# Channel attention with a routed expert layer on one core: squares of the next batch's first products behind the third routing step's row numbers, and its bias table one routing step earlier

## The chip, the cores and the metric

The kernel runs on one core of a Trainium2 chip. The metric is the device time of one execution in microseconds (us), from launch to end. The kernel before has three timed runs: 1178.34, 1178.45 and 1178.51 us, a median of 1178.45 us. A further execution was recorded by the hardware profiler; all rows of the trace below come from it.

The engines of the core are named as the profile names them: PE multiplies matrices (PEld is its loading of weights), DVE and ACT work element by element, POOL starts the indirect DMAs, and SP starts all other DMAs. Each engine has a queue of its own instructions, and engines wait for each other through semaphores.

## What is computed

The reference is a channel attention over four batches, followed by a mixture of eight experts with one expert for each token. Cut to what matters:

```python
# q, k, v: (4, 5056, 256)
qn = q / (norm(q, axis=1) + 1e-6);  kn = k / (norm(k, axis=1) + 1e-6)
a = softmax(kn.transpose(0, 2, 1) @ qn / tau)      # (4, 256, 256)
x = (v @ a).reshape(20224, 256)
logits = x @ w_gate + modality_bias[modality_id]   # 8 experts
e_idx = argmax(logits); gate = softmax(logits)[e_idx]
out[t] = gate[t] * (relu(x[t] @ w1[e]) @ w2[e])    # e = e_idx[t], hidden size 1024
```

## The kernel before

A batch's 5056 tokens are cut into ten steps of 512 tokens (the last is shorter). Three kinds of work run over these steps.

**Products.** For each batch the 256x256 product k'q is summed in one PSUM tile (`g`, L368) over the ten steps, from loads of q and k. Beside it the squares of q and k are summed for the norms: ACT squares a half step into `sq` (L347), DVE adds it to `acc` (L349). In a step there are four such pairs, q and k of two halves. A function `kq_pieces(b, s, behind, later)` hands out one step. With a list given as `later`, the squares aren't put out there and then but collected in that list, and are put out when the main loop runs the list; and with `behind`, each of them is ordered on its engine behind the instructions that `behind` names. Batch 0's product fills the first 45 us; batch 1's steps are spread over batch 0's routing steps, and so on.

**Routing steps.** There are 40, numbered g = 0 to 39, ten in a batch. A step turns v (L570 on PE for the first six steps; a DMA that transposes, L537 into `T`, then four DMAs into planes `pl`, L514, and joining copies into `vt`, L521 and L522, for the later ones), splits it into a high and a low part (`vh` on ACT, L574; `vl` on DVE, L575), multiplies it by the attention in four tiles of 128 tokens (`xp`, L588), copies the result into rows `x` (L595, L599, L600) and adds the bias table `bsel` to the logits (L601). Then DVE finds each token's expert, PE makes prefix sums over the tokens (`rp`, L646 and L647), and DVE works out each token's row number (`pi`, L660). POOL scatters the rows into a DRAM buffer `xs` that is sorted by expert, four indirect DMAs a step (L477). The scatters of steps 3 and 4 are held until the fourth tile of the next step has been copied (`HELD`).

**Blocks.** A block is 512 rows of one expert, and there are 40 here. After each routing step from g = 2 on (except one) DVE picks a block from the counts (`pick`, L700 to L730). Its weights are loaded on SP (`w1r`, `w2r`, two halves each), its rows are read back from `xs` by a transposing DMA (`Tx`, L769), joined into `xt` (L521, L522) and split into `xh` (ACT, L833) and `xl` (DVE, L834). PE multiplies by w1 (`hp`, L848) and w2 (`y`, L869), each as three products of high and low parts. Block 0 (called slot 0) needs the rows of steps 0, 1 and 2; `START = 2` is the index of the last of these.

What sets the order: the Python loops hand out pieces, a helper deals the pieces of several streams out in proportion, and when the program is built a scheduler lays each engine's instructions out in one fixed order, by when it reckons each to be ready. `order(ins, others)` adds that one instruction stands behind others on its queue. On the chip, each queue keeps that order.

Around the change: batch 1's product steps 0 and 1 are put out before routing step 0, step 2 beside routing step 1. Their squares in the kernel before: step 0's at once; step 1's after routing step 0, behind its row numbers (`routed[0]`: on DVE the numbers at L660 and the gate at L666, on ACT the copy of the token numbers at L662); step 2's after routing step 1, behind `routed[1]`. `setup_bias` makes a batch's bias table from the modality of each token in three operations on DVE (L262 twice, L267); for batch 1 it is put out after routing step 7 (`NS // 2 + 2` with NS = 10), behind that step's numbers.

Of the kernel before, what the change touches and what calls it, by code (L numbers as in the profile page):

```python
# [20 lines left out]
def _interleave(*streams):  # L21

    lists = [list(s) for s in streams if len(s) > 0]
    total = [len(x) for x in lists]
    at = [0] * len(lists)
    while any(a < n for a, n in zip(at, total)):
        i = min(
            (i for i in range(len(lists)) if at[i] < total[i]),
            key=lambda i: ((at[i] + 0.5) / total[i], i),
        )  # L30
        lists[i][at[i]]()
        at[i] += 1
# [3 lines left out]
def kernel(  # L36
# [15 lines left out]
    B, N, C = q.shape  # L52
# [4 lines left out]
    NS = -(-N // STEP)  # L57
# [19 lines left out]
    START = 2  # L77
# [103 lines left out]
    def pad_rows():  # L181

        ins = nc.sync.dma_start(
            xs[E * CAP : E * CAP + BLK, :].rearrange("(p t) c -> p t c", t=BLK // P),
            pad[0].bitcast(I32).unsqueeze(1).to_broadcast([P, BLK // P, XW]),
        )
        pads.append(ins.ins)
        tc.declare_no_dep(
            ins.ins, group="xr", reason="no expert has rows there"
        )  # L190
# [283 lines left out]
    routed = {}  # L474
# [20 lines left out]
    def slots_by(g):  # L495

        return max(0, g + 1 - START - sum(x <= g for x in SKIP))

    def lag(g):

        n = LAG
        for x in SKIP:
            n -= g >= x + n
        return n
# [424 lines left out]
    def run(pieces):  # L929
        for f in pieces:  # L930
            f()
# [19 lines left out]
    def once(blk, what):  # L951
        key = (blk["slot"], what)
        if key not in done:
            done.add(key)
            run(blk[what])

    def block_stream(blk, nxt):

        once(blk, "load")
        once(blk, "prep")  # L960
        body = list(blk["body"])
        if nxt is not None:
            once(nxt, "load")
            done.add((nxt["slot"], "prep"))
            split0, turn, split1 = nxt["prep"]
            for o, f in reversed(list(zip((7, 10, 13), (split0, lambda: turn(blk["evicted"][NJ - 3]), split1)))):
                body.insert(o, f)
        before = open_blk[0]["last"] if open_blk[0] is not None else []
        for i, f in enumerate(open_blk[0]["stores"] if before else []):
            blk["beside"].setdefault(2 + i, []).append(f)  # L970
        open_blk[0] = blk
        if not before:
            return [blk["first"]] + body
        return [blk["first"], before[0], body[0]] + before[1:] + body[1:]
# [17 lines left out]
    def ask(n):  # L992
        if n < len(tasks) and n not in loaded:
            loaded.add(n)
            product(n)[0]()

    def products_of(g):

        out = []
        for n, (at, b, i) in enumerate(tasks):  # L1000
            if at == g:
                out += [lambda n=n: ask(n)] if g <= first_block else []
                out += product(n)[1:]
                if g >= first_block and (b, i) != (1, NS - 1):
                    out.append(lambda n=n: ask(n + (1 if g == first_block else 2)))
        if g == first_block + 1:
            out.append(lambda: ask(min(n for n in range(len(tasks)) if tasks[n][0] > g) + 1))
        return out
# [1 line left out]
    va = [va_pieces(*divmod(g, NS)) for g in range(G)]  # L1010
    va[0][2]()
    run(va[0][0])
    squares = {1: [], 2: []}
    for s in BEFORE:
        if s == 0:
            run(kq_pieces(1, s))
        else:
            run(kq_pieces(1, s, lambda: routed[0], squares[s]))
    pad_rows()
    for g in range(G):  # L1020
        b, s = divmod(g, NS)
        streams = []
        for gg, blk in waiting:
            if gg <= g + 1 - lag(g + 1):
                once(blk, "load")
        if len(waiting) > 0 and waiting[0][0] <= g - lag(g):
            _, blk = waiting.pop(0)
            streams.append(block_stream(blk, waiting[0][1] if waiting and waiting[0][0] <= g + 1 - lag(g + 1) else None))
        soft = list(softmax_pieces(b)) if s == 0 and b > 0 else []
        begun = []  # L1030
        if g + 1 == first_block:
            split0, turned, split1 = waiting[0][1]["prep"]
            done.add((0, "prep"))
            begun = [split0, split1]
        own = list(va[g][1])
        if g - 1 in HELD:
            t = HELD[g - 1]
            own.insert(t + 1, lambda: va[g - 1][4]([copied[g, t]]))
        turn = []
        if g + 1 < first_block:  # L1040
            turn.append(va[g + 1][2])
        turn += va[g + 1][0] if g + 1 < G else []
        if g + 1 == first_block:
            turn.append(va[g + 2][2])
        if g == first_block:
            turn.append(va[g + 2][2])
        if first_block <= g + 2 < G:
            turn.append(va[g + 2][3])
        if g + 3 == first_block or first_block + 2 < g + 3 < G:
            turn.append(va[g + 3][2])  # L1050
        if g < first_block:
            streams.append(soft + turn + begun + own)
        else:
            streams.append(soft + own[:2] + turn[:1] + own[2:5] + turn[1:] + own[5:])
        if b + 1 < B:
            if b == 0 and s == 1:
                streams.append(list(kq_pieces(1, 2, lambda: routed[1], squares[2])))
            else:
                streams.append(products_of(g))
        _interleave(*streams)  # L1060
        if waiting and waiting[0][0] <= g + 1 - lag(g + 1):
            blk = waiting[0][1]
            once(blk, "load")
            if blk["slot"] == 0:
                turned(blk["evicted"][-1])
            once(blk, "prep")
        if s == NS // 2 + 2 and b < B - 1:
            setup_bias(b + 1, routed[g])
        n = slots_by(g)
        while chosen < n:  # L1070
            waiting.append((g, block_pieces(g, chosen, pick(g, chosen, False), False)))
            chosen += 1
        run(squares.get(g + 1, []))
        if g == NS - 1:
            ask(min(n for n in range(len(tasks)) if tasks[n][0] > g) + 1)
# [84 lines left out]
```

## Time and profile before

| what | value |
|---|---|
| time, median of 3 runs | 1178.45 us |
| time of the profiled execution | 1175.55 us |
| span of the profiled execution, first to last instruction | 1173.7 us |
| PE busy | 1153.6 us (98%) |
| DVE busy | 920.8 us (78%) |
| ACT busy | 806.1 us (69%) |
| POOL busy | 384.7 us (33%) |
| granted TensorE clock, mean | 0.995 |

The span leaves out 1.85 us of the profiled execution's time (1175.55 less 1173.7), and that execution took 2.9 us less than the median run. A difference in the span is carried over to the median as it is. In the rows, "start" and lengths are in us, counted from the first instruction; brackets give how long the engine was idle before the row and what ended that. A busy PE isn't a PE at full speed, since a matmul's time includes waiting in the pipeline; how many matmuls start in a stretch tells more. The clock that PE was granted is in a row of its own, in tenths.

### The profile page before, as it was taken

The numbers are of one execution on the slowest core, as the hardware profiler recorded it, in microseconds if no ns is written. First come the engines' busy times: TensorE is split into PE (matmuls) and PEld (weight loads), VectorE is DVE, ScalarE is ACT, GpSimd is POOL, SyncE is SP. The second block draws the span as 40 slices with busy tenths as digits, with TensorE's granted clock in tenths as the row PEclk, the third lists the DMA queues.
The fourth block names the chain that finished last, engine by engine and source line by source line (L and its number), as shares of the span: only waits on it lengthen the run. The fifth ranks groups of instructions, "written<-read, shape, count | busy, mean of one in ns | idle before, by whom it ended". The sixth has DMA issues, their size and how long they took to land.

```text
span 1173.7 us, 23358 instructions
## 1 busy us (share of the span) xinstructions
PE 1153.6 (98%) x7708; PEld 1054.6 (90%) x7708; DVE 920.8 (78%) x2591; ACT 806.1 (69%) x1655; POOL 384.7 (33%) x345
## 2 busy tenths in 40 slices
PE   8998999999999999999999999999999999999997
PEld 7896989999999999999999999999999999999997
DVE  6787989898888888888888888878777776686552
ACT  6676867877777777687777677767656666556553
POOL 0053333323333332333333333333333333344122
PEclk9998999999999999999999999999999999999999
DMA  8979999688777677759777776765876665464421
GB/s 293 307 236 230 269 239 255 173 248 217 199 200 201 196 192 206 208 159 234 204 209 203 210 202 162 167 182 158 207 218 172 187 176 158 134 178 136 136 86 35
DMA packets 285843, 228.38 MB, mean 195 GB/s; under 512 B 185064, under 2 KB 243944, under 8 KB 285712
## 3 DMA queue, kind: packets, MB, share of 16 engines
q1 hardware_dynamic: 270032, 185.19, 60.3%
q0 software_dynamic: 15680, 41.61, 10.4%
q8 instruction: 62, 1.02, 0.4%
q14 instruction: 69, 0.57, 0.2%
HBM read 128.79 MB, written 43.43 MB: 147 GB/s over the span
## 4 chain that ended last, share of the span: by engine, by line
PE 84%; issue 6%; DMA 5%; POOL 2%; DVE 2%; ACT 1%; SPq 0%; POOLq 0%; DVEq 0%; ACTq 0%
PE y L869 34%; PE hp L848 33%; PE xp L588 9%; PE g L368 6%; DMA k<-in_k_dram 2%; POOL out_dram L477 2%; DMA q<-in_q_dram 1%; DMA Tx<-xs 1%; DMA xs<-x,pi 0%; DMA pl<-T 0%; PE vtp L570 0%; PE gw L437 0%; ACT xt L521 0%; SPq L305 0%; PE atp L431 0%
## 5 line engine op out<-in xcount | busy, mean ns | idle before, releaser
L869 PE MATMUL y<-w2h,hh 128*128 128x256 f32 x1256 | 354.5, 282 | 0.0
L869 PE MATMUL y<-w2l,hh 128*128 128x256 f32 x1256 | 351.2, 280 | 0.0
L869 PE MATMUL y<-w2h,hl 128*128 128x256 f32 x1256 | 349.4, 278 | 0.1
L477 POOL DMA_INDIRECT xs<-x,pi x160 | 196.7, 1229 | 364.0 <-DVE pr L711 183.4
L477 POOL DMA_INDIRECT out_dram<-yo,gt x158 | 174.2, 1103 | 392.1 <-ACT hh L851 297.6
L848 PE MATMUL hp<-xh,w1h 128*128 128x512 f32 (+1 forms) x640 | 250.7, 392 | 5.6 <-ACT xh L833 5.6
L848 PE MATMUL hp<-xl,w1h 128*128 128x512 f32 (+1 forms) x640 | 250.7, 392 | 0.0
L848 PE MATMUL hp<-xh,w1l 128*128 128x512 f32 (+1 forms) x640 | 249.5, 390 | 0.0
L852 DVE SCALAR_TENSOR_TENSOR hl<-hp,hh 128x512 fp32r<-128x512 f32 (+1 forms) x320 | 216.7, 677 | 36.3 <-ACT hh L851 34.6
L869 PEld LDWEIGHTS y<-w2h,hh 128*128 128x128 f32 x1256 | 236.4, 188 | 9.3
L869 PEld LDWEIGHTS y<-w2l,hh 128*128 128x128 f32 x1256 | 236.4, 188 | 8.5
L851 ACT ACTIVATE hh<-hp 128x512 fp32r<-128x512 f32 (+1 forms) x320 | 188.7, 590 | 69.2 <-PE hp L848 69.0
L869 PEld LDWEIGHTS y<-w2h,hl 128*128 128x128 f32 x1256 | 235.3, 187 | 0.4 <-DVE hl L852 0.3
L814 ACT CAST w1h<-w1r 128x512 fp32r<-128x512 f32 x160 | 99.4, 621 | 166.4 <-PE hp L848 165.6
L821 DVE TENSOR_TENSOR w1l<-w1r,w1h 128x512 fp32r<-128x512 f32 x160 | 109.8, 686 | 91.1 <-ACT w1h L814 90.4
L848 PEld LDWEIGHTS hp<-xh,w1l 128*128 128x128 f32 x640 | 120.6, 188 | 26.0
L848 PEld LDWEIGHTS hp<-xh,w1h 128*128 128x128 f32 x640 | 120.4, 188 | 19.5 <-ACT xh L833 5.8
L848 PEld LDWEIGHTS hp<-xl,w1h 128*128 128x128 f32 x640 | 120.8, 189 | 13.4
L821 DVE TENSOR_TENSOR w2l<-w2r,w2h 128x512 fp32r<-128x512 f32 x160 | 109.8, 686 | 12.6 <-ACT w2h L814 11.3
L814 ACT CAST w2h<-w2r 128x512 fp32r<-128x512 f32 x160 | 100.8, 630 | 21.7 <-PE y L869 20.1
L588 PE MATMUL xp<-ah,vh 128*128 128x264 f32 x320 | 92.7, 291 | 0.1
L600 DVE COPY x<-xp 128x256 uint16<-128x256 uint16 x136 | 56.9, 419 | 45.5 <-ACT x L599 45.1
(161 smaller groups left out, 1817.1 us busy)
## 6 DMA issues: line engine op xcount, KB each, us to landing
w1r<-in_moe_w_dram SPq DMA_DIRECT2D x80, 512.0 KB, 4.7
w2r<-in_moe_w_dram SPq DMA_DIRECT2D x80, 512.0 KB, 4.6
q<-in_q_dram SPq DMA_DIRECT2D x35, 512.0 KB, 9.4
k<-in_k_dram SPq DMA_DIRECT2D x35, 512.0 KB, 5.5
pl<-T SPq DMA_DIRECT2D x120, 128.0 KB, 4.6
v<-in_v_dram SPq DMA_DIRECT2D x6, 512.0 KB
xs<-x,pi POOLq DMA_INDIRECT x160, 4.8
out_dram<-yo,gt POOLq DMA_INDIRECT x158, 3.2
```

Of the source, the lines that this page charges most:

```text
L368: nc.tensor.matmul(gram[b][:, m, :], x, y, start=first and m == 0 and i == 0, stop=last and i == len(seq) - 1, skip_group_check=True,)
L477: ins = nc.gpsimd.indirect_dma_start(out=dst, out_offset=bass.IndirectOffsetOnAxis(ap=idx, axis=0), in_=rows, in_offset=None, bounds_check ...
L588: nc.tensor.matmul(xp[:, 0:DE], a[:, h, t * P : (t + 1) * P], w[:, h, :], start=i == 0, stop=i == len(seq) - 1,)
L600: copied[g, t] = nc.vector.tensor_copy(planes[:, 0, :], halfwords[:, 0, :]).ins
L814: ins = nc.scalar.copy(hi, src).ins
L821: evicted[-1] = [ins, nc.vector.tensor_tensor(lo, src, hi.bitcast(F32), ALU.subtract).ins]
L848: nc.tensor.matmul(hp[:, 0:rows], w[:, h, fs], x[:, h, 0:rows], start=i == 0, stop=i == len(seq) - 1)
L851: relu = nc.scalar.activation(hh[:, 0:rows], hp[:, 0:rows], AF.Relu).ins
L852: low = nc.vector.scalar_tensor_tensor(hl[:, 0:rows], hp[:, 0:rows], 0.0, hh[:, 0:rows].bitcast(F32), ALU.max, ALU.subtract).ins
L869: ins = nc.tensor.matmul(y, a[:, tsl], w[:, j % 2, :], start=(j == 0 and i == 0 and t % per == 0), stop=(j == NJ - 1 and i == 2), skip_gro ...
```

## The change

Three places of the main program are edited. The squares of batch 1's product steps 1 and 2 go into one list that is run after routing step 2 (`START`), and all eight pairs are ordered behind step 2's numbers in place of step 0's and step 1's. Batch 1's bias table is put out after routing step 6 in place of step 7; the other batches' stay.

```diff
-    squares = {1: [], 2: []}
+    squares = {START + 1: []}
     for s in BEFORE:
         if s == 0:
             run(kq_pieces(1, s))
         else:
-            run(kq_pieces(1, s, lambda: routed[0], squares[s]))
+            run(kq_pieces(1, s, lambda: routed[START], squares[START + 1]))
...
             if b == 0 and s == 1:
-                streams.append(list(kq_pieces(1, 2, lambda: routed[1], squares[2])))
+                streams.append(list(kq_pieces(1, 2, lambda: routed[START], squares[START + 1])))
...
-        if s == NS // 2 + 2 and b < B - 1:
+        if s == (NS // 2 + 1 if b == 0 else NS // 2 + 2) and b < B - 1:
             setup_bias(b + 1, routed[g])
```

No instruction is added or taken away on any engine. But the scheduler lays out the stretch from routing step 0 to the fourth block anew, so more moves than the diff names. Three places matter below. In the names, the numbers behind a tile are first what it belongs to and last a running number of the build (`rp_2` is routing step 2's, `xp_3_0` is tile 0 of step 3, `pl_7` and `vt_7` are step 7's planes and their joined copy, `Tx_0`, `xt_0` and `xh_0` belong to slot 0, `hl_1_0` to slot 1, `bsel_1` and `btmp_1` to batch 1).

On PE, step 2's prefix sums stood in this place, within the fourth tile of step 3:

```order
L588 MATMUL xp_3_3_915<-ah_0_440,vh_3_749 128x264
L588 MATMUL xp_3_3_915<-al_0_441,vh_3_749 128x264
L646 LDWEIGHTS trim_93
L646 MATMUL rp_2_819<-chosen_of_98,trim_93 128x40
L588 MATMUL xp_3_3_915<-ah_0_440,vl_3_750 128x264
L647 LDWEIGHTS onesb_86
L647 MATMUL rp_2_819<-run_2_814,onesb_86 128x40
```

and now they stand behind the first tile of step 3:

```order
L588 MATMUL xp_3_0_884<-ah_0_440,vl_3_726 128x264
L368 MATMUL g_1_487<-q_1_3_860,k_1_3_862 128x256 x2
L646 LDWEIGHTS trim_93
L646 MATMUL rp_2_795<-chosen_of_98,trim_93 128x40
L368 MATMUL g_1_487<-q_1_3_860,k_1_3_862 128x256
L647 LDWEIGHTS onesb_86
L647 MATMUL rp_2_795<-run_2_790,onesb_86 128x40
```

Seventeen matmuls of step 3 and most of the product matmuls of batch 1's step 3 have moved behind the prefix sums.

On ACT, where slot 0's rows are joined and split, the order was

```order
L521 COPY xt_0_0_1270<-Tx_0_1133 128x512
L521 COPY xt_0_1_1275<-Tx_0_1133 128x512
L595 COPY x_5_991<-xp_5_3_1206 128x512
L833 CAST xh_0_1268<-xt_0_0_1270 128x512
L662 COPY x_5_991<-tokid_100 128x4
L833 CAST xh_0_1268<-xt_0_1_1275 128x512
```

and is now

```order
L521 COPY xt_0_0_1270<-Tx_0_1133 128x512
L521 COPY xt_0_1_1275<-Tx_0_1133 128x512
L521 COPY vt_7_0_1394<-pl_7_1157 128x512
L595 COPY x_5_991<-xp_5_3_1206 128x512
L662 COPY x_5_991<-tokid_100 128x4
L833 CAST xh_0_1268<-xt_0_0_1270 128x512
L833 CAST xh_0_1268<-xt_0_1_1275 128x512
```

A copy of routing step 7's planes has come in ahead of slot 0's split. Before, it stood 13 instructions behind the second `xh`. On SP the DMAs from slot 0's `Tx` to these planes stand in the same order in both kernels.

On DVE, the bias table stood behind step 7's numbers, seventeen instructions ahead of the low halves (`qs`, L324) of batch 1's product step 6:

```order
L660 TENSOR_REDUCE pi_7_2044<-pos_7_2041 128x4
L262 SCALAR_TENSOR_TENSOR bsel_1_2072<-m1_131,mb_sb_263 128x320
L262 SCALAR_TENSOR_TENSOR btmp_1_2073<-m1_131,mb_sb_263 128x320
L711 SCALAR_TENSOR_TENSOR pr_5_2078<-pr_5_2078,prio9_115 128x9
L575 TENSOR_TENSOR vl_9_2216<-vt_9_0_2219,vh_9_2215 128x512
L267 TENSOR_TENSOR bsel_1_2072<-bsel_1_2072,btmp_1_2073 128x320
```

and now stands behind step 6's, among the sums of squares of product step 4:

```order
L660 TENSOR_REDUCE pi_6_1634<-pos_6_1631 128x4
L262 SCALAR_TENSOR_TENSOR bsel_1_1662<-m1_131,mb_sb_263 128x320
L262 SCALAR_TENSOR_TENSOR btmp_1_1663<-m1_131,mb_sb_263 128x320
L705 TENSOR_TENSOR pr_4_1668<-end9_124,nxt9_121 128x9
L349 TENSOR_TENSOR acc_1_488<-acc_1_488,sq_1_4_0_k_1685 128x2x256
L267 TENSOR_TENSOR bsel_1_1662<-bsel_1_1662,btmp_1_1663 128x320
```

The three operations have moved 64 instructions forward on DVE.

## The prediction

> **What bounds the kernel now.** I read the page's slices first, which show PE full nearly everywhere, then busy times by stretch around the slices that fall short, then PE's waits, then the chain of waits around the one place where PE stops. The busy times (start and end, length, then busy us and count for PE, PEld, DVE, ACT, POOL, then granted clock, DMA share, GB/s):
>
> ```profile
> 54.00:92.90 38.90, 38.73 (x263) 35.10 (x261) 31.21 (x142) 28.41 (x63) 16.46 (x16) 1.00 0.73 213
> 92.90:105.00 12.10, 6.52 (x23) 4.88 (x22) 5.27 (x31) 5.10 (x12) 4.36 (x4) 0.72 1.05 250
> 105.00:200.00 95.00, 93.17 (x631) 84.80 (x630) 86.17 (x239) 75.78 (x156) 34.26 (x26) 1.00 1.03 257
> 200.00:1085.00 885.00, 884.92 (x6019) 811.40 (x6018) 717.92 (x2019) 620.53 (x1278) 308.06 (x267) 1.00 0.70 190
> ```
>
> From 200 to 1085 us PE is never idle, so what happens earlier shifts the end one to one: a microsecond at the first block is a microsecond of the time. PE's own waits between 40 and 200 us (total, times, longest) name the two that count:
>
> ```profile
> PE hp L848 <- ACT xh L833: 5.6, 1, 5.6
> PE g L368 <- DVE qs L324: 1.6, 2, 1.1
> ```
>
> The first is slot 0's start, the second comes at 155 to 160 us. The chain of waits leads to the first:
>
> ```profile
> 57.21 0.87 PE vtp L570 x8
> 58.08 1.45 PE xp L588 x12
> 59.53 0.43 PE g L368 x2
> ...
> 68.39 0.44 PE vtp L570 x4
> 68.82 3.46 PE g L368 x16
> ...
> 72.52 0.72 PE xp L588 x6
> ...
> 82.39 5.62 DMA xs<-x,pi
> ...
> 98.62 1.22 PE hp L848 x2
> ...
> 100.50 3.41 PE hp L848 x8
> ```
>
> PE's matmuls pace routing step 2 (the six at 72.52 are its fourth tile), its scatters follow, slot 0's rows come back through `Tx`, and `hp` starts at 98.62.
>
> **Step 2's numbers come earlier.** The sums stood in DVE's queue right behind step 0's and step 1's numbers:
>
> ```profile
> 57.86 0.17 DVE L601 TENSOR_TENSOR L<-xp,bsel 128x8 f32<-128x8 f32 x1 [0.75 <-ACT x L595]
> ...
> 60.85 0.21 DVE L660 TENSOR_REDUCE pi<-pos 128x4 int32<-128x32 f32 x1
> 60.98 0.68 DVE L349 TENSOR_TENSOR acc<-acc,sq_q 128x512 f32<-128x512 f32 x1
> ...
> 77.56 0.20 DVE L660 TENSOR_REDUCE pi<-pos 128x4 int32<-128x32 f32 x1
> ```
>
> Eight sums at 0.60 from start to start are 4.8 us of DVE, and they go behind the last of these rows. But PE set the pace, so I count PE. From 59.53 to the end of step 2's fourth tile (72.52 + 0.72 = 73.24) it took 13.7 us. In the new order 16 product matmuls (3.46 by the row at 68.82), 36 of `xp` (1.45 / 12 = 0.121 each, 4.36), 8 transposes (0.88) and two prefix pairs (0.23 each, an estimate from the chain's 0.43 for two product matmuls) stand in between: 9.15, so the tile ends at 68.7. From there to the numbers step 0 took 61.06 - 57.21 = 3.85 (its fourth tile ended where the chain goes on with the transposes; a copy and the L row follow), with one low half in between as here. So step 2's numbers are done at 72.55 instead of 77.76, 5.2 us earlier. If DVE still lags by a low half or two, it is 4.0; if the prefix sums wait for nothing, 5.6.
>
> The scatters follow on POOL, 0.78 behind the numbers' end:
>
> ```profile
> 78.54 0.98 POOL L477 DMA_INDIRECT xs<-x,pi  x1 [3.58 <-ACT x L662]
> ```
>
> They start 1.28 apart (the chain's 82.39 is the fourth), and by the same count step 1's have left POOL by 72.7, so nothing stands in front. The load of q and k for product step 5 reuses the buffer of step 1, now waits for step 1's squares (some 72 us by this count), and holds its place on SP ahead of slot 0's weights; it needs 1 MB of the DMA engines in a stretch that has room (0.73 above). I cost it at nothing, and at 1 us if that room is gone. `Tx` is then issued at 83.5 instead of 88.72.
>
> **But ACT has a new wait ahead of `xh`.** ACT's queue now holds the copy of step 7's planes between `xt_0` and `xh_0`. What that copy waits for stands on SP behind `Tx`, in the same order as before:
>
> ```profile
> 88.72 2.43 SPq L769 DMA_TRANSPOSE Tx<-xs  x1
> ...
> 93.08 5.84 SPq L537 DMA_TRANSPOSE T<-in_v_dram  x1
> ...
> 101.05 2.65 SPq L514 DMA_DIRECT2D pl<-T  x4
> ```
>
> ```profile
> 97.48 0.57 ACT L595 COPY x<-xp 128x512 uint16<-128x512 uint16 x1
> 97.94 0.62 ACT L833 CAST xh<-xt 128x512 fp32r<-128x512 f32 x1
> 98.46 0.20 ACT L662 COPY x<-tokid 128x4 int32<-128x4 int32 x1
> 98.56 0.62 ACT L833 CAST xh<-xt 128x512 fp32r<-128x512 f32 x1
> ...
> 108.07 0.76 ACT L521 COPY vt<-pl 128x512 uint16<-128x512 uint16 x1
> 108.70 0.62 ACT L347 ACTIVATE sq_q<-q 128x512 f32<-128x512 f32 x1
> ```
>
> The copy needs the third and fourth of the plane DMAs, which started at 102.4 and 103.0; the trace has their landing at
>
> ```profile
> DMA to landing us min/median/max: 4.5/5.1/5.8
> ```
>
> so not ahead of 107.5, and at 108.07 ACT read them without a wait. I take 107.8: 19.1 us behind `Tx`'s issue. In the new order that is 83.5 + 19.1 = 102.6. Then come the copy (0.63 to the next row), `x` (0.46), the token numbers (0.10) and `xh` to `hp` (98.62 - 97.94 = 0.68): `hp` starts at **104.5 instead of 98.62, 5.9 us later**. Behind the waiting copy on ACT stand also `x_5` (on which the held scatters of step 4 wait) and all of slot 0's relu; on DVE the logits of step 5. What is late next after the gain of 5.2 is thus the planes, by far: `Tx` itself would allow 93.4. ACT does stand still for planes already, in the waits from 105 to 200:
>
> ```profile
> ACT vt L521 <- DMA pl<-T: 4.9, 2, 2.8
> ```
>
> The unknown is how long `T` takes to land with its surroundings changed. From its issue to the first plane DMA it was 5.6 (55.12 to 60.73), 8.0 (93.08 to 101.05) and 10.5 (111.00 to 121.46):
>
> ```profile
> 55.12 3.18 SPq L537 DMA_TRANSPOSE T<-in_v_dram  x1
> ...
> 60.73 0.65 SPq L514 DMA_DIRECT2D pl<-T  x1
> ```
>
> ```profile
> 111.00 5.99 SPq L537 DMA_TRANSPOSE T<-in_v_dram  x1
> ...
> 121.46 2.58 SPq L514 DMA_DIRECT2D pl<-T  x4
> ```
>
> I take 8.0, the row in the same place, and keep -2.4 and +2.5 for the range. `T` is half a megabyte. The Trainium skill ("DMA: Bandwidth & Descriptors", Latency and other measured facts) gives transposing DMAs 261 GB/s. By that the half megabyte would need an estimated 2 us, `hp` would start some 6 us sooner than in my sum, and the change would come out near no change. The rows, at three to five times that, don't bear it out; it is weighed with the second rival.
>
> **The slow start after the gap.** The eight `hp` matmuls at 100.50 take 3.41 us, 0.43 each. At full clock it is 0.23:
>
> ```profile
> 108.48 1.38 PE hp L848 x6
> ```
>
> Twelve or so go at the slow rate after the gap, which costs 2.4 us. The gap grows here, but the ramp is paid once either way, so I put it at nothing. The Trainium skill ("TensorE: Matmul & The Clock Gate", Part 1) has the clock halve after an idle window of about 3.4 us and come back after as much sustained work, whatever the idle time. By that rule the ramp would go only where the gap falls under that window, which is the first rival's case; the granted 0.72 in the second row of the busy times agrees with it.
>
> **The bias table.** Its three operations stood just where PE waits for `qs`:
>
> ```profile
> 151.79 0.48 DVE L262 SCALAR_TENSOR_TENSOR bsel<-m,mb_sb 128x320 f32<-128x320 f32 x1
> 152.19 0.48 DVE L262 SCALAR_TENSOR_TENSOR btmp<-m,mb_sb 128x320 f32<-128x320 f32 x1
> ...
> 153.28 0.48 DVE L267 TENSOR_TENSOR bsel<-bsel,btmp 128x320 f32<-128x320 f32 x1
> 156.06 0.67 DVE L324 TENSOR_TENSOR qs<-q,qs 128x512 fp32r<-128x512 f32 x1
> ```
>
> Without them `qs` comes 1.2 us sooner (3 x 0.40 from start to start), off a wait of 1.6 us. I take -1.2. At most the 1.6 go; at worst the three delay a low half of slot 1 by 1.2 where DVE is nearly full (86.17 of 95), which would give +1.2.
>
> **The sum.** +5.9 - 1.2 = +4.7 on a span of 1173.7. Carried to the median of the runs, 1178.45 (the profiled execution itself has 1175.55), that is 1183.1. Ends: 5.9 - 0.4 - 2.4 - 1.6 = +1.5, and 5.9 + 1.2 + 1.0 + 2.5 + 1.2 = +11.8, if all ends meet.
>
> **Rivals.**
> - *The planes aren't late, and the gain of step 2 goes through.* It decides at 96.7: planes that land by then leave `hp` no later than before. Then `hp` starts between 93.4, where `Tx` allows it and PE's earlier work just ends, and about 96, since the eight sums now delay steps 3 and 4; the ramp of 2.4 may go too. With the bias that is -3.8 to -8.8; I take -6, 1172.4. For it speaks that the scheduler put the copy there as ready; against it, that `T` is issued behind `Tx` and no row has planes landing sooner than 10.1 after `T`'s issue (5.6 + 4.5), which from `T` at 87.9 gives 98. Chance 0.08.
> - *The wait is there but short.* `T` lands in 5.6 as in its first row, the planes in 4.5: `hp` 2.9 later, less 1.2 for the bias, +1.7, 1180.2: within 0.2%. 0.14, the skill's rate included.
> - *It goes on.* The held scatters of step 4 start behind `x_5` at about 104, the last of them 3.9 later, and with 5.6 to land like the chain's they are there at 113; `Tx` of slot 2, which needs them, now stands on SP ahead of q and k for product step 6, so SP stands still until then. If that and a slow `T` (+2.5) add up, +9, 1187.5. 0.06.
>
> **How the numbers follow.** The forecast has 0.72; the likeliest time is its 1183.1. About 0.2%, or 2.4 us, is what a measurement of this kernel tells from no change. Slower by more than that: 0.72 + 0.06 = 0.78; within it 0.14; faster 0.08. The range of 8 in 10 leaves out the first rival and the very ends: 1179.5 (the short wait) to 1187.5.
>
> **What would show it.** In the new profile: step 2's `pi` at 72.5, `Tx` issued at 83.5, ACT idle for some 10 us with `vt <- pl` behind it, PE waiting for `xh` until 104.5 with a clock of 0.7 or less, and the `qs` wait under 0.6. Wrong would be: `Tx` not earlier (then the sums were never in the way, and the loss nears 10), planes landed ahead of `xt`, or a new PE wait after 105.

## The result, and the profile after

The changed kernel takes 1185.63 us, the median of six runs (1184.35 to 1187.87); the kernel before, timed beside it, takes 1178.48 us (six runs, 1174.66 to 1178.67). The ratio is 1.0068, with a 95% interval of 1.0053 to 1.0083: slower, by 7.15 us from median to median. The profiled execution of the changed kernel took 1185.73 us with a span of 1183.9, which is 10.2 us more than the span before.

First PE's waits between 40 and 400 us in the changed kernel (total, times, longest):

```profile
PE hp L848 <- ACT x L662: 7.1, 1, 7.1
PE rp L646 <- DVE chosen_of L622: 3.6, 2, 2.6
PE xp L588 <- issue: 2.5, 2, 2.2
PE rp L647 <- DVE run L632: 0.5, 1, 0.5
```

The wait for `qs` is gone, as foretold. The wait ahead of `hp` is there and larger. Two new ones stand before it in time: `rp`, for 1.0 us in routing step 2 and 2.6 in step 4, and `xp` in step 2 (`issue` means that the profile shows nothing the engine waited for; `remote`, further down, that it doesn't know who ended the wait). The chain from `Tx` to `hp` on SP, ACT and PE (start, length, engine, line; in brackets the idle time before the row and what ended it):

```profile
89.92 2.29 SPq L769 DMA_TRANSPOSE Tx<-xs  x1
...
95.11 4.59 SPq L537 DMA_TRANSPOSE T<-in_v_dram  x1
...
103.90 2.60 SPq L514 DMA_DIRECT2D pl<-T  x4
...
108.95 0.76 ACT L521 COPY vt<-pl 128x512 uint16<-128x512 uint16 x1 [9.56 <-DMA pl<-T]
109.58 0.57 ACT L595 COPY x<-xp 128x512 uint16<-128x512 uint16 x1
...
110.28 1.13 ACT L833 CAST xh<-xt 128x512 fp32r<-128x512 f32 x2
...
110.95 1.22 PE L848 MATMUL hp<-xh,w1h 128*128 128x512 f32 x2 [7.05 <-ACT x L662]
```

ACT stands still for 9.56 us with step 7's planes copy at the head of its queue and slot 0's `xh` behind it. `hp` starts at 110.95 instead of 98.62, 12.3 us later. But `Tx` was to be issued earlier than before, at 83.5, and is issued 1.2 us later, at 89.92. Step 2's numbers are the reason:

```profile
78.27 0.21 DVE L660 TENSOR_REDUCE pi<-pos 128x4 int32<-128x32 f32 x1
```

They end at 78.48, where 72.55 was forecast and the kernel before had 77.76. PE lost the time on the way. Busy times by stretch, in the columns of the prediction, of the changed kernel:

```profile
66.00:78.00 12.00, 8.49 (x51) 7.35 (x49) 5.07 (x22) 6.02 (x14) 4.94 (x6) 0.86 0.44 137
...
100.00:112.00 12.00, 4.95 (x21) 4.44 (x21) 3.28 (x21) 3.02 (x8) 2.37 (x4) 0.50 0.90 221
```

and of the kernel before in the first of these stretches:

```profile
66.00:78.00 12.00, 11.97 (x86) 11.05 (x86) 10.08 (x49) 8.90 (x23) 5.18 (x5) 1.00 0.69 227
```

In the 12 us from 66 on, PE started 51 matmuls instead of 86, DVE was busy for half as long and ACT for two thirds. No engine was full there. PE, ACT and POOL of the changed kernel around that gap:

```profile
66.62 0.28 PE L588 MATMUL xp<-ah,vl 128*128 128x264 f32 x1
...
68.08 0.28 PE L588 MATMUL xp<-ah,vl 128*128 128x264 f32 x1
70.52 0.39 PE L588 MATMUL xp<-ah,vh 128*128 128x264 f32 x1 [2.16 <-issue]
```

```profile
69.68 0.58 ACT L595 COPY x<-xp 128x512 uint16<-128x512 uint16 x1 [2.83 <-PE xp L588]
72.53 0.58 ACT L595 COPY x<-xp 128x512 uint16<-128x512 uint16 x1 [2.27 <-PE vtp L570]
74.00 1.07 ACT L595 COPY x<-xp 128x512 uint16<-128x512 uint16 x2 [0.88 <-PE vtp L570]
```

```profile
62.33 1.15 POOL L477 DMA_INDIRECT xs<-x,pi  x1 [51.02 <-DVE pi L660]
...
71.48 0.98 POOL L477 DMA_INDIRECT xs<-x,pi  x1 [0.30 <-issue]
```

and POOL of the kernel before, where step 1's scatters begin:

```profile
69.85 1.27 POOL L477 DMA_INDIRECT xs<-x,pi  x1 [2.71 <-DVE acc L349]
```

The matmul at 66.62 is the last of step 2's first tile, and it ends at 66.90. ACT had been idle for 2.83 us when it began to copy that tile at 69.68. The next two tiles ended at 67.64 and 68.36 and were copied at 72.53 and 74.00, with ACT idle before each. In steps 0 and 1 such a copy starts 0.04 us behind its last matmul. Here three copies in a row are 2.8, 2.3 and 0.9 us late, counted from the tile's end or, where ACT was still busy, from when it came free (the expectations below count from when ACT could have started its next copy, and have 2.4 and 1.0). PE can't go on until the tiles are free, and so lies idle too. The trace's semaphore events say the same of the signals themselves: PE's signals for the three tiles reached the counter at 69.66, 72.51 and 73.97, and three more, of matmuls that ended at 71.52, 72.19 and 73.05, followed from 74.05 to 74.17. The ends of matmuls are modelled in the profile, so it can't be told whether the results were late or only the signals; "late signals" below stands for both. Beside it, POOL issues eight scatters without a pause, those of steps 0 and 1, from 62.33 to 72.46. In the kernel before there were four, a pause of 2.7 us, and four more.

The table sets the places that count side by side for all kernels of this study (end of step 2's numbers, `Tx` of slot 0 issued, first `hp`, span, all in us of one profiled execution; the ratio is that of the timed runs to the kernel before on the same chip). Its median there was 1177.27 us beside the runs from bias_alone to step2_alone, 1177.52 beside those down to before_step0_held and 1175.26 beside the last four, each group on another chip, so kernels of different groups are compared by their ratios and not by their times. One of the twelve runs of bias_planes9 took 1975.24 us at a granted clock of 0.655, and the ratio leaves it out.

| kernel | numbers | `Tx` | `hp` | span | ratio (95%) |
|---|---|---|---|---|---|
| before | 77.76 | 88.72 | 98.62 | 1173.7 | 1 |
| after | 78.48 | 89.92 | 110.95 | 1183.9 | 1.0068 (1.0053 to 1.0083) |
| bias_alone | 77.63 | 88.46 | 96.56 | 1176.5 | 1.0014 (1.0003 to 1.0025) |
| squares_alone | 78.39 | 89.92 | 110.00 | 1184.9 | 1.0079 (1.0066 to 1.0092) |
| planes_behind_hh | 77.97 | 89.49 | 103.92 | 1184.6 | 1.0052 (1.0038 to 1.0067) |
| step2_alone | 73.94 | 84.94 | 99.22 | 1175.8 | 1.0014 (1.0005 to 1.0023) |
| step1_held | 72.57 | 85.41 | 107.25 | 1181.4 | 1.0054 (1.0041 to 1.0067) |
| planes_both | 77.62 | 89.09 | 103.17 | 1182.8 | 1.0060 (1.0047 to 1.0073) |
| held_and_planes | 74.01 | 86.62 | 98.96 | 1178.0 | 1.0049 (1.0030 to 1.0067) |
| before_step0_held | 82.80 | 93.70 | 103.26 | 1180.6 | 1.0051 (1.0031 to 1.0070) |
| all_planes9 | 73.86 | 86.45 | 98.64 | 1181.1 | 1.0044 (1.0030 to 1.0058) |
| before_planes9 | 77.93 | 88.89 | 96.66 | 1174.8 | 1.0000 (0.9987 to 1.0013) |
| bias_planes9 | 77.54 | 88.42 | 96.24 | 1175.6 | 1.0009 (0.9996 to 1.0023) |
| step2_planes9 | 73.59 | 84.29 | 92.77 | 1177.4 | 1.0020 (1.0010 to 1.0029) |

### The profile page after: what moved, and what is told of

Its sections match the earlier page's. It is cut to its first block, busy times and chain, and to the rows that moved or that the text cites. A ratio compares the mean times of both kernels' runs of the same rounds, so it can differ in the third digit from the quotient of the medians.

```text
span 1183.9 us, 23369 instructions
## 1 busy us (share of the span) xinstructions
PE 1156.4 (98%) x7708; PEld 1057.6 (89%) x7708; DVE 921.8 (78%) x2591; ACT 808.1 (68%) x1655; POOL 391.0 (33%) x345
## 3 DMA queue, kind: packets, MB, share of 16 engines
q0 software_dynamic: 15680, 41.61, 10.2%
## 4 chain that ended last, share of the span: by engine, by line
PE 86%; issue 7%; POOL 2%; ACT 2%; DMA 2%; DVE 2%; POOLq 0%; SPq 0%; ACTq 0%; DVEq 0%
PE y L869 33%; PE hp L848 33%; PE g L368 9%; PE xp L588 9%; POOL out_dram L477 2%; DMA T<-in_v_dram 1%; ACT x L595 0%; PE vtp L570 0%; DMA k<-in_k_dram 0%; DMA xs<-pad,pki 0%; PE gw L437 0%; ACT yo L883 0%; DMA pl<-T 0%; DVE vl L575 0%; PE atp L431 0%
## 5 line engine op out<-in xcount | busy, mean ns | idle before, releaser
L477 POOL DMA_INDIRECT xs<-x,pi x160 | 202.8, 1267 | 369.7 <-DVE pr L711 190.4
```

The costliest lines, as they stand in the source:

```text
L477: ins = nc.gpsimd.indirect_dma_start(out=dst, out_offset=bass.IndirectOffsetOnAxis(ap=idx, axis=0), in_=rows, in_offset=None, bounds_check ...
```

## The experiments

**The two parts apart.** First the bias table alone, in the kernel before:

```diff
-        if s == NS // 2 + 2 and b < B - 1:
+        if s == (NS // 2 + 1 if b == 0 else NS // 2 + 2) and b < B - 1:
```

> The kernel before with batch 1's bias table put out behind routing step 6, and the squares left where they were. If the prediction's term D is right, the wait of PE for qs at about 142 us (1.6 us before) falls to under 0.6, nothing else in the first 130 us changes by more than 0.3 us, and the time is 1.0 to 1.6 below the kernel before: about 1177.1. If the wait is ended by something that stands behind the table, it only changes its name: within 0.4 of the kernel before. If the three DVE operations come ahead of something more urgent behind step 6, the time is 0.5 to 1.5 above.

The time was 1178.79 us, 1.0014 of before. PE's wait for `qs` (which stood at 155 to 160 us in the kernel before, not at 142) did fall from 1.6 to 0.2 us, and other waits for `hl` stand in the list, 2.9 us of them at 151.4 to 154.3:

```profile
PE hp L848 <- DVE hl L852: 4.4, 3, 2.9
...
PE g L368 <- DVE qs L324: 0.2, 1, 0.2
```

```profile
151.69 0.76 ACT L521 COPY vt<-pl 128x512 uint16<-128x512 uint16 x1 [4.62 <-DVE bs L651]
152.32 0.60 ACT L814 CAST w1h<-w1r 128x512 fp32r<-128x512 f32 x1
152.84 0.59 ACT L851 ACTIVATE hh<-hp 128x512 fp32r<-128x512 f32 x1
```

ACT stands still for 4.62 us ahead of the copy of step 9's planes, with a relu of slot 1 behind it. So the wait for `qs` went as expected, and the expected gain in time didn't come. The waits for `hl` offer themselves as what took it, which is tried at the end of this section.

Then the squares alone, the changed kernel with the old place of the bias table:

> The change without its second edit: the squares of steps 1 and 2 behind step 2's numbers, the bias table behind step 7 as before. If term D has its size also in the changed kernel, where the first product comes about 12 us later, the qs wait of 1.6 is back and the time is 1 to 1.6 above the changed kernel, about 1187.0. If the later first product had already covered the table, the time is that of the changed kernel, 1185.6 to within 0.5. In both cases the instructions up to 130 us are those of the changed kernel, so this is also a second look at the place where term A failed: if PE's standing still between 68.4 and 70.5, and the late evictions of step 2's tiles at 69.7, 72.5 and 74.0, come from the order, step 2's numbers end near 78.5 again and Tx is issued near 90; if they were a chance of one execution, the numbers end near 72.5 to 74 and Tx is issued near 84 to 85.

1186.65 us, 1.0079: the squares carry the whole loss, and the same late copies and the same late `Tx` (89.92) are in its trace, so they are no accident of one execution. That the bias table is worth some 1 us within the change (1.0079 against 1.0068) fits the forecast of 1.2, but the two intervals overlap.

**The wait for the planes.** The copy of step 7's planes is ordered behind the third relu of slot 0 on ACT, and behind its low half on DVE (`made` collects each block's relus and low halves as they are built):

```diff
-                    [cast[g - 1]] if g == first_block else (),
+                    [cast[g - 1]] if g == first_block else made[-1] if g == first_block + 1 else (),
...
-            evicted[j] = [relu, low]
+            evicted[j] = [relu, low]; made.append(evicted[j])
```

> The change with one ordering edge more: the copy of step 7's first planes stands on ACT behind the third eviction of slot 0's first product, where it stood in the kernel before; PE's, SP's and POOL's orders stay those of the changed kernel. By the prediction's term B, ACT goes from xt straight to xh: the first product starts 2 to 3 us after xt, at about 100.4 if Tx is issued at 89.9 again, in place of 110.95, and the time falls by 8 to 10.5, to 1175.5 to 1178. If the cost of the change came from the scatters and the transfers and not from ACT's queue, hp starts early but PE then waits elsewhere by as much, and the time stays over 1183.

`hp` started at 103.92, 7.0 us sooner than in the changed kernel and without a wait, but the time was 1184.03 us, 1.0052, against 1.0068: some 1.9 us less, and the two intervals overlap. So it is the second of the two cases expected. In the trace PE and ACT then wait at the next planes, those of step 8:

```profile
PE y L869 <- ACT yo L883: 5.0, 1, 5.0
```

```profile
139.02 0.76 ACT L521 COPY vt<-pl 128x512 uint16<-128x512 uint16 x1 [8.44 <-DMA pl<-T]
139.66 0.60 ACT L814 CAST w1h<-w1r 128x512 fp32r<-128x512 f32 x1
140.17 0.59 ACT L851 ACTIVATE hh<-hp 128x512 fp32r<-128x512 f32 x1
```

It is the same wait one step on. On SP these planes are issued at 128.58, behind slot 2's `Tx` (121.73); in the kernel before they went at 121.46, ahead of that `Tx` (132.13).

**Only step 2's squares.** Step 1's squares stay where they were, behind step 0's numbers; step 2's squares and the bias table are as in the change:

```diff
-    squares = {START + 1: []}
+    squares = {1: [], START + 1: []}
...
-            run(kq_pieces(1, s, lambda: routed[START], squares[START + 1]))
+            run(kq_pieces(1, s, lambda: routed[0], squares[1]))
```

> The change with step 1's squares left behind step 0's numbers as before; only step 2's squares stand behind step 2's, and the bias table behind step 6. On ACT the copy of step 7's first planes stands behind xh here, but its half on DVE stands ahead of both xl of slot 0, and hp's second matmul reads xl. If a wait for the planes costs the same on whichever queue it stands, hp's first matmul starts 2 to 3 us after xt and the second one waits for the planes, 19 us after Tx was issued: the time is 1182 to 1187. If only ACT's queue counts, the time is 1175 to 1179.

1178.35 us, 1.0014: most of the loss is gone, against the first expectation. Step 2's numbers came at 73.94, 3.8 us sooner than before, and slot 0's `hp` all the same at 99.22. The gap had only moved. In this kernel the eight scatters of steps 1 and 2 run together, from 70.84 to 81.55, and the late copies stand there:

```profile
78.78 0.59 ACT L595 COPY x<-xp 128x512 uint16<-128x512 uint16 x1 [4.11 <-PE vtp L570]
81.02 0.59 ACT L595 COPY x<-xp 128x512 uint16<-128x512 uint16 x1 [1.66 <-remote]
```

PE had finished the first of these tiles at 74.77. That made a theory: a run of eight scatters without a pause keeps PE's signals from the engines that wait for them. The next two kernels try it from both sides.

**The run of eight taken apart.** In the changed kernel step 1's scatters are held back as those of steps 3 and 4 are:

```diff
-    HELD = {3: 3, 4: 3}
+    HELD = {1: 3, 3: 3, 4: 3}
```

> The change with step 1's four scatters held back until step 2's fourth tile is copied off PSUM, so that no longer eight of them follow each other without a pause between 62 and 72.5; the orders on PE, ACT, DVE and SP stay. Theory S: in the changed kernel the eight scatters in a row are what makes ACT see PE's finished tiles 2.8, 2.4 and 1.0 us late at 66.9 to 74. Then the three evictions start within 0.1 of their matmuls' end, PE has no pause between 68.4 and 70.5, step 2's numbers end at 72 to 74 in place of 78.5, step 3's at 84 to 88 in place of 91, and the time falls by 3 to 6, to 1180 to 1183. Theory O: the lateness belongs to the order of PE and ACT with the squares gone; then step 2's numbers end near 78.4 again, and the time is 1184.5 to 1187.

Step 2's numbers came at the forecast time, and PE was full in the stretch that had the gap:

```profile
72.36 0.21 DVE L660 TENSOR_REDUCE pi<-pos 128x4 int32<-128x32 f32 x1
```

```profile
66.00:78.00 12.00, 11.93 (x79) 10.77 (x78) 10.27 (x39) 9.10 (x20) 7.97 (x6) 1.00 0.81 244
```

They end at 72.57; the prediction had 72.55. The three copies are 0.5, 0.3 and 0.0 us late. The time fell less than theory S had it: 1182.97 us, 1.0054 against 1.0068, with intervals that overlap. The wait for the planes is still there, and larger:

```profile
105.25 0.76 ACT L521 COPY vt<-pl 128x512 uint16<-128x512 uint16 x1 [11.73 <-DMA pl<-T]
```

**The run of eight put into the kernel before.** Step 0's scatters are held until step 1's fourth tile is copied, and nothing else is edited:

```diff
-    HELD = {3: 3, 4: 3}
+    HELD = {0: 3, 3: 3, 4: 3}
```

> The kernel before, with step 0's four scatters held until step 1's fourth tile is copied, so that steps 0 and 1 make eight in a row from about 66 to 76 where the kernel before pauses 2.7 us. By theory S some of ACT's evictions between 70 and 77 start 0.6 to 4 us after their matmuls' end, where all of them start within 0.1 in the kernel before, and the time rises by 1 to 5. By theory O none is late by over 0.2, and the time rises by 0 to 2, by the later scatters alone.

1182.83 us (two runs), 1.0051: 5.3 us, just over what theory S allowed. POOL, ACT and PE:

```profile
65.52 1.16 POOL L477 DMA_INDIRECT xs<-x,pi  x1 [54.36 <-DVE L L601]
...
74.70 0.98 POOL L477 DMA_INDIRECT xs<-x,pi  x1 [0.30 <-issue]
```

```profile
77.18 0.59 ACT L574 CAST vh<-vtp 128x512 fp32r<-128x512 f32 x1 [7.22 <-remote]
```

```profile
72.51 0.49 PE L570 MATMUL vtp<-ident,v 128*128 128x128 f32 x3
...
78.61 0.59 PE L588 MATMUL xp<-ah,vh 128*128 128x264 f32 x1 [4.02 <-DVE L L601]
```

PE's transposes ended at 73.0, and ACT, idle for 7.22 us, began to read them at 77.18, 1.5 us behind the last of the eight scatters (75.68). By the semaphore events, six signals of matmuls that ended between 71.7 and 74.6 all arrived from 77.07 to 77.39. The same stall stands in a kernel that has none of the change, only the run of eight, with the order of all instructions on every engine that of the kernel before, and step 2's numbers came 5.0 us late. So neither the moved squares nor their place on DVE are needed for it. That the run of eight by itself is enough is not shown, as the last kernel below and the last section tell.

**Both mended, and the planes after them.** Three more kernels follow the time that didn't come back. The first adds to planes_behind_hh that slot 2's `Tx` stands behind step 8's planes on SP:

```diff
-                after(ins.ins, padded)
+                after(ins.ins, padded); order(ins.ins, parted[f"pl_{first_block + 2}"] if slot == 2 else ())
```

(`parted` collects the plane DMAs of L514.)

> The run before with the planes' copy behind the third eviction, and one ordering edge more: on SP the transfer of slot 2's rows (Tx) stands behind step 8's planes, as in the kernel before, where the change had put it ahead of them. Theory: with step 7's planes out of the way, the loss came back at step 8's, because SP issued them at 128.6 behind that Tx (121.5 in the kernel before) and ACT waited 8.4 us for them at 130 to 139. With the edge pl of step 8 is issued at 122 to 126 and ACT's wait falls to 0 to 3; what is left is the lateness of hp (5 us) less what the bias table gives: the time is 1179.5 to 1182. Rival: the planes of step 8 wait for T of step 8 or for its buffer and not for SP; then they are issued at 127 or later all the same, and the time stays at 1183 to 1185.

1184.15 us, no gain over planes_behind_hh. Step 8's planes are read at 134.17, 4.9 us sooner, and the wait turns up at step 9's: ACT idle for 5.71 us until 157.91, PE for 2.9. The second has all three edits, with step 1's scatters held too:

> The last two together: step 1's scatters held, step 7's planes copied behind the third eviction, step 8's planes ahead of slot 2's rows on SP. If the late signals (theory S) and the two waits for planes are all that the change costs, the first product starts at or before the kernel before's 98.6 and the time is 1173.5 to 1178: at or under the kernel before. If the squares behind step 2's numbers cost by themselves (step 3's numbers 4 us or more later than the 81.7 of the kernel before, since PE's and DVE's work of 66 to 78 comes between), the time is 1178 to 1182.

1181.14 us, 1.0049. Of the two cases expected it is the second: step 3's numbers end at 86.56, 4.8 us behind the 81.72 of the kernel before, and the time lies in the range given for it. So the squares behind step 2's numbers seem to cost by themselves. What that does to the transfers behind it, and how much of the waits below comes from it, wasn't taken apart. Up to 124 us this kernel runs level with the kernel before (`hp` at 98.96, 0.3 us later). Then it loses at step 8's and at step 9's planes:

```profile
129.92 0.77 ACT L521 COPY vt<-pl 128x512 uint16<-128x512 uint16 x1 [4.35 <-DVE pk L724]
...
153.84 0.76 ACT L521 COPY vt<-pl 128x512 uint16<-128x512 uint16 x1 [6.28 <-DVE pos L654]
```

```profile
156.46 0.50 PE L848 MATMUL hp<-xh,w1h 128*128 128x512 f32 x1 [3.95 <-DVE hl L852]
```

The brackets of these two copies, and of the one at 151.69 in bias_alone, name DVE instructions that make nothing for a copy. That the copies wait for their planes is read from the last of the plane DMAs, which was issued 6.8 and 5.6 us ahead of them here, 7.1 us in bias_alone, and 5.5 us ahead of step 9's copy in the kernel before.

The third also puts step 9's planes behind the last relu of slot 1:

```diff
-                    [cast[g - 1]] if g == first_block else made[-1] if g == first_block + 1 else (),
+                    [cast[g - 1]] if g == first_block else made[-1] if g == first_block + 1 else made[2 * NJ - 1] if g == first_block + 3 else (),
```

> held_and_planes with one edge more: the copy of step 9's first planes stands behind the last eviction of slot 1's first products (hh and hl number 7) on ACT and DVE. Theory P: what was won before 130 us is taken back at 147 to 154, where ACT and DVE wait 6.3 us for step 9's planes with hl queued behind them, and PE 3.9 us for hl. Then that wait of PE goes, and the time falls by 2 to 4 below held_and_planes, to 1177 to 1179. Rival: step 9's own tiles are what is late; then PE waits for them (xp of step 9, or its numbers) instead, and the time stays within 1 of held_and_planes, at 1180 to 1182.

1181.0 us, 1.0044. The wait came out at step 8's planes again, whose copy starts at 135.22 behind 8.73 us of idle ACT. PE's wait for `hl` fell from 3.9 to 1.2 us, and one of 6.0 for `yo` (L883) came in its place. So the expectation that step 9's copy was the last thing in the way was wrong.

**The order of step 9's copy alone** was then tried in three kernels that don't have the large wait: the kernel before, the kernel before with the bias table moved, and step2_alone. The edit on each is

```diff
-                    [cast[g - 1]] if g == first_block else (),
+                    [cast[g - 1]] if g == first_block else made[2 * NJ - 1] if g == first_block + 3 else (),
```

> The kernel before with that same one edge for step 9's planes and nothing else. In its trace ACT waits 2.8 us for these planes at 146 to 149, but PE's only wait there is the 1.6 us for qs, so by theory P alone the time stays within 1 of the kernel before (1176.5 to 1178.5).

1174.89 us, 1.0000 (0.9987 to 1.0013): no change, as expected.

> bias_alone with the edge for step 9's planes. If the bias table's 1.6 us was really gained at qs and lost again at hl behind step 9's planes (theory P), the time is 1 to 2.5 below bias_alone (1178.8), and 0 to 1.6 below before_planes9. If the table behind step 6 costs by itself, the time stays at 1178 to 1180.

1177.4 us, 1.0009 (0.9996 to 1.0023). Against bias_alone's 1.0014 the intervals overlap, and against before_planes9 on the same chip, where 0 to 1.6 us less were expected, it is 2.5 us more, with intervals that overlap too. So whether the wait at 151 us ate the bias table's gain isn't settled, and no gain over the kernel before can be seen.

> step2_alone with the edge for step 9's planes. By theory P the 1.3 us that step2_alone loses between 125 and 150 (hh number 9 to 16) goes: 1176.5 to 1178. If step 9's tiles are late themselves, the time is step2_alone's 1178.3 to within 0.7.

1177.81 us, 1.0020: no better than step2_alone, and a miss. `hp` now starts as early as 92.77, but PE then waits 10.9 us for `xl` in the same slot. Its trace also holds a counterexample. Ahead of step 9's copy every engine has the same instructions in the same order as in step2_alone, and POOL runs the same eight scatters of steps 1 and 2 without a pause:

```profile
70.50 0.98 POOL L477 DMA_INDIRECT xs<-x,pi  x1 [3.19 <-ACT vh L574]
...
80.23 0.98 POOL L477 DMA_INDIRECT xs<-x,pi  x1 [0.30 <-issue]
```

```profile
75.80 0.58 ACT L595 COPY x<-xp 128x512 uint16<-128x512 uint16 x1 [0.75 <-PE xp L588]
```

Here the copy that came 1.7 us late in step2_alone (81.02) starts 0.04 us behind the end of its tile (75.76), and the one ahead of it is as punctual. A run of eight is thus not enough; something that can differ between two executions of the same order belongs to it. The two traces do differ in one thing, the semaphore events that they hold (last section).

No kernel of this study beats the kernel before.

## Why the prediction was right and wrong

The median of 1185.63 lies in the range, on the forecast side, 2.5 us above the forecast of 1183.1. The wait that it named is there; that the number came so close is in part luck, as the last point works out. By its own steps:

- **"Step 2's numbers come earlier" failed in the changed kernel.** Its count of PE's work was right: step1_held, where PE isn't held up, has them at 72.57. What it left out is the stall of PE and ACT between 66.9 and 74. Step 1's scatters, which move forward with everything else, now follow step 0's without a pause; I had counted that they would have left POOL by 72.7 (they had, by 72.46), but didn't ask what happens beside them while they run. The runs tie the stall to these eight, though not to them alone (last section). The numbers are 5.9 us later than forecast, and `Tx` was issued at 89.92 instead of 83.5: 6.4 us, the whole miss at `hp` (110.95 less 104.5).
- **Two more errors in the same step nearly cancel.** The four scatters of step 2 were to take 0.98 each; one of them took 4.91 (last section), 3.9 us more. And from the start of the fourth to `Tx` it was 2.9 us (87.03 to 89.92), where the kernel before, from which I took it, has 6.3 (82.39 to 88.72). So the 6.4 us are 5.9 + 3.9 - 3.4. In step1_held, where the numbers are on time, one scatter took 4.96 and `Tx` was issued only at 85.41.
- **"ACT has a new wait ahead of `xh`" was right, and its size too.** The planes were read 19.0 us behind `Tx`'s issue (108.95 less 89.92) where 19.1 was forecast, and 19.8 in step1_held. What was wrong is what I took to follow from it. "A microsecond at the first block is a microsecond of the time" holds in neither direction once the wait is taken away: planes_behind_hh brings `hp` 7.0 us forward and the ratio only from 1.0068 to 1.0052; held_and_planes starts `hp` where the kernel before does and is still 1.0049; before_planes9 and bias_alone start it 2 us sooner than the kernel before's trace and gain nothing. In the traces of the mended kernels the next waits are for the planes of steps 8 and 9, and step 3's numbers are late wherever all eight squares stand behind step 2's.
- **The slow clock was put at nothing, and on the path to the end that held.** The granted clock behind each `hp` start, before and after:

```profile
98.60:102.00 3.40, 3.38 (x9) 2.81 (x10) 3.36 (x18) 1.35 (x5) 2.79 (x3) 0.50 0.94 193
102.00:106.00 4.00, 4.00 (x22) 3.08 (x21) 1.60 (x9) 2.38 (x6) 1.29 (x2) 0.76 0.98 325
```

```profile
110.90:115.00 4.10, 4.05 (x11) 3.38 (x12) 3.17 (x16) 2.34 (x6) 3.19 (x4) 0.50 1.08 217
115.00:120.00 5.00, 5.00 (x29) 3.96 (x29) 3.52 (x16) 4.15 (x9) 1.68 (x2) 0.90 1.16 261
```

  Both start at 0.50 and climb back within some 8 us. Other slow stretches are new (0.86 from 66 to 78, and 0.50 from 100 on, both above), but they lie ahead of `hp`, which waits for the planes and not for PE.
- **The bias table** did what was forecast at its place: the wait for `qs`, 1.6 us, is gone. From `hp` (12.3 us late) to the end (10.2 late) the changed kernel made good 2.1 us, against 1.2 in the sum. As an edit by itself it is worth nothing (bias_alone).
- **"It goes on", the third rival,** was there in part. Slot 2's `Tx` did go ahead of q and k and of step 8's planes on SP (122.62 against 126.69 and 130.04). In the changed kernel ACT waits only 1.8 us for these planes, behind the larger wait; in planes_behind_hh, without the larger one, it waits 8.4.
- **The sum and its carrying over.** The span grew by 10.2, not 4.7. "Wrong would be: `Tx` not earlier ..., and the loss nears 10" is what the trace shows, though not for the reason given there: the sums were in the way, and something else took their place. The medians differ by 7.15 only, since the profiled execution of the kernel before (1175.55) was 2.9 us quicker than its median and that of the changed kernel was not. "Carried to the median" as it is, the trace's 10.2 would have given 1188.6. So the small distance of 2.5 us is a miss of 5.5 less an error of 3.0 the other way, which is luck.

## What to carry to other kernels

When a piece of work moves forward, look at what each queue then runs without a pause, and not only at whether the queue is free in time: the pause that goes may have been what its neighbours needed. Where a queue's order puts a copy that waits for a late transfer ahead of work on the path, price the transfer from its issue, and look for the next copy of the same kind behind it, since mending the first wait may only uncover the second. Before a gain at one place is counted as time, ask which transfer is the next limit, and compare one profiled execution with the spread of the timed runs before carrying its difference over. Before a stall is put down to an order of instructions, see that the traces compared hold the same share of their events.

## What the runs showed of the hardware

- **PE's signals came late beside long runs of scatters.** The profiles of after, squares_alone, planes_behind_hh, planes_both and before_step0_held all have eight scatters in a row at step 2, and there a reading on ACT that is 2.3 to 4.2 us late; step2_alone has both at step 3 (4.0 us), step2_planes9 has the run and no late copy. With step 1's scatters held (step1_held, held_and_planes, all_planes9) step 2's copies are at most 0.7 us late, though steps 1 and 2 then make a run of eight, beside which one copy of step 3 is 2.0 us late in step1_held, 0.3 in held_and_planes and none in all_planes9. With four in a row, the kernel before and two like it have every copy of steps 0 to 5 within 0.04 us, and bias_alone has one 0.5 and one 1.3 us late. So long runs and late signals go together in most traces, and taking a run apart or making one moved the stall as expected.
- **A second condition goes with the late signals in every trace.** In nine of the fourteen traces, those of the changed kernel and of the first two groups of runs, about a tenth of the semaphore events of PE, ACT and DVE is missing from the record: the changed kernel's holds 838 for the 928 instructions of PE that signal. In the other five, those of the kernel before and of the last group, hardly one is missing (927 for 927 in the kernel before). Each of the nine has a copy in steps 0 to 5 that is 0.5 us late or more, and the five have none over 0.04, though all_planes9 and step2_planes9 among them run eight scatters in a row. Three pairs of kernels have the same order on every engine up to 125 us or more: the kernel before and bias_alone, held_and_planes and all_planes9, step2_alone and step2_planes9. In each pair only the trace with missing events has late copies. In these steps, readings over 1.5 us late are found only where missing events and a run of eight come together, and not in all of these (held_and_planes has 0.7 at most). Whether the chip, the recording or something else is the second condition, and what holds the signals back, stays open. No trace of the changed kernel with all its events exists, nor one of the kernel before with events missing, so part of the difference between those two traces may not come from the change. The ratios compare runs on one chip each, and the changed kernel's 1.0068 and before_step0_held's 1.0051 are losses over several runs; whether they would stand on the chip of the last group wasn't tried.
- **A scatter beside eight sums in a row takes 4.9 us instead of 0.98.** POOL and DVE of the changed kernel:

```profile
80.53 4.91 POOL L477 DMA_INDIRECT xs<-x,pi  x1 [0.30 <-issue]
...
87.03 0.98 POOL L477 DMA_INDIRECT xs<-x,pi  x1 [0.30 <-issue]
```

```profile
79.61 0.67 DVE L349 TENSOR_TENSOR acc<-acc,sq_q 128x512 f32<-128x512 f32 x1
...
83.91 0.67 DVE L349 TENSOR_TENSOR acc<-acc,sq_k 128x512 f32<-128x512 f32 x1
84.51 0.67 DVE L575 TENSOR_TENSOR vl<-vtp,vh 128x512 fp32r<-128x512 f32 x1
```

  It begins among the sums and ends at 85.44, 0.9 us behind the last of them and 0.3 behind the low half that follows, and it comes back with 4.9 to 5.0 us in the six other kernels that put eight sums in a row beside a scatter. The kernel before, with four sums (68.97 to 71.47), had 1.27. The Trainium skill ("SBUF — State Buffer", section "SBUF: two separate sides") says that a DMA issued by GpSimd (POOL here) can't have its descriptors written while DVE runs an operation in a mode that holds the port pair they share. The rows agree with such a lock for the eight sums and show little of it for the four; no run here tells whether these sums hold it throughout.
- **One wait for planes followed another.** From 100 to 140 us the DMA engines' share was 0.9 to 1.2 in the changed kernel and 1.06 to 1.18 in the kernel before, and each kernel that removed one wait for planes got another. Whether the transfers' bytes, their order on SP or the two together set when planes of steps 8 and 9 arrive stays open.
